# Magnitude tables as products of sixteen exponentials, a split of two long VectorE operations, late PSUM banks and new weights in a planner that orders a fused kernel on one core

## The chip, the cores and the metric

The kernel runs on one core of one Trainium2 chip. The metric is the device time of one execution in microseconds (us). A profile of one execution gives for every engine which instruction ran when: TensorE (PE, with its weight loads apart as PEld), VectorE (DVE), ScalarE (ACT), GpSimd (POOL, unused here) and SyncE (SP, which issues all DMAs of this kernel in one queue).

## The reference

The reference mixes two branches over one input x (2048 tokens, 512 channels), all in float32:

```python
g = sigmoid((x * gate_w).sum(-1, keepdims=True))
# a: a convolution along the tokens with a kernel K of length L = 2048 per channel d
dt   = exp(log_dt)[:, None]
P    = exp((dt * (A_re + 1j * A_im))[:, :, None] * arange(L))        # 512 x 128 x 2048
K    = einsum("dn,dnl,dn->dl", C, P, dt * B).real
a    = irfft(rfft(u padded to 2L) * rfft(K padded to 2L))[:L] + u * Dskip
# b: a gated MLP, hidden width 1792
b    = (sigmoid(x @ w_gate) * (x @ w_up)) @ w_down
out  = g * a + (1 - g) * b
```

What the change touches most is P. With the token index written as l = 32 i + j, each of the 512 x 128 complex powers is a product of a value at a multiple of 32 and a value at a small step, so K comes out of small matmuls over the 128 states instead of out of 512 x 128 x 2048 exponentials.

## The kernel before

**The MLP** takes most of TensorE. The tokens are worked in two halves of 1024, each in two blocks of 512; the hidden width in 14 slices of 128, in groups of 4, 4, 3 and 3. Inputs and weights are split into a high and a low part (`split`, L678: ACT copies the high part, DVE subtracts it, through four staging buffers `st`), and each product is three matmuls in float32r. `hidden` (L731) makes 24 matmuls a slice and block into two PSUM banks (`gups`, L749); `post` (L760) is the chain behind them: sigmoid on ACT (L764), product on DVE (L766), high part on ACT (L770), low part on DVE (L771). `down` (L782) multiplies by `w_down` (`dps`, L798), and `add` (L808) adds the result into an accumulator, on ACT for the first group (L814) and on DVE after (L817).

**The kernel K** is made in 16 groups of 32 channels, one after the other. `bases` (L281) computes for a group: the angles (DVE L315, ACT L317, DVE L318, ACT L331), cosine and sine (ACT L332 and L333) into the tile `ex`, five exponentials a channel and state on ACT for the doubling steps (`e5`, L334), and the magnitudes `mg` = exp(aa * q) for q = 0..63, a table of 32 x 64 values a partition. These are 32 ACT instructions, one a channel, with the channel's decay as a per-partition scale (`mags`, L336 to L338). `tables` (L365) then multiplies `mg` and `ex` into the table B (DVE L389 with 2048 elements, L392 and L393 with 1024), builds the table T by five doublings on DVE (L350 to L361), and 64 small matmuls (`kps`, L409) give K. `first` (L418) takes the first step of K's transform (ACT L422, DVE L425, matmuls `wps` L434, ACT L446) and stores every two groups (`a_k`). The tiles `ex`, `mg`, T and B have one buffer each, so the next group's `bases` starts when B is built, and T is refilled when the small matmuls have read it.

**The convolution** is a transform in steps: `rows` (L461) transforms the input and stores it (`a_u`); `passes` (L519) runs over two halves of the channels, each as soon as its eight groups of K are stored, with 16 steps (`step`, L543: matmuls `s2u` and `s2k`, products on DVE, matmuls `ips`, a store to `b_s`); `finals` and `last` (L602, L618) load `b_s` back, finish the transform (matmuls `fps`) and add it to the MLP's accumulator (DVE L640 and L647), from which the output is stored.

**The order of the work** is not written out. All these functions are generators ("strands"), each of which yields one operation at a time with its engine, a price and the times when its inputs are ready, and `Plan.run` (L150) merges them while the program is built: it keeps a clock for every engine, and always issues the operation with the smallest key, which is its possible start on that clock plus the strand's weight ("bias").

```python
                    start = max(ready, self.free.get(eng, 0.0))
                    key = start + st[0]
```

The prices are formulas: `dve(n)` = 0.067 + n x 1.042e-3 us and `act(n)` = 0.06 + n x 0.88e-3 us for n elements a partition. The merge decides the order on each engine for good; on the chip each engine works its instructions off in that order and waits where an input is late. A PSUM bank (three are shared by everything but the MLP, `XB`) is taken when the strand asks for it, which it does before its matmuls' inputs are ready.

Of the kernel before, what the change touches and what calls it, by code (L numbers as in the profile page):

```python
# [31 lines left out]
P = 128  # L32
# [6 lines left out]
NA = len(ANGLES)  # L39
GROUPS = [4, 4, 3, 3]  # L40
HALF = L // 2
LN2H, LN2L = 0.693145751953125, 1.42860682030941723212e-6
WIDTHS = [256, 256]


def constants():
# [15 lines left out]
    for k in range(32):  # L62
# [11 lines left out]
        "c_pw": f(np.concatenate([ANGLES, ANGLES[33:], np.arange(64)]), 1, NA + 69),  # L74
# [23 lines left out]
def slots(pool, tag, n, shape, dtype=F32):  # L98
    return [Slot(pool, f"{tag}{i}", shape, dtype) for i in range(n)]


class Plan:
# [47 lines left out]
    def run(self):  # L150
        while True:
            best = None
            i = 0
            while i < len(self.strands):
# [20 lines left out]
            if eng == "SP":  # L175
# [17 lines left out]
            fn(eng) if isinstance(st[2][0], tuple) else fn()  # L193
# [3 lines left out]
def body(ctx, tc, xp, xt, prm, ldt, dsk, gw, wgu, wdn, c_wu, c_wf, c_wk, c_ww, c_pw, out):  # L197
# [26 lines left out]
    GU, DN, XB = (slots(ps, n, k, [P, 512]) for n, k in (("gu", 3), ("dn", 2), ("xb", 3)))  # L224
# [6 lines left out]
    pw = cst.tile([P, NA + 69], F32, name="pw")  # L231
# [49 lines left out]
    def bases():  # L281
# [3 lines left out]
        for gi in range(NG):  # L285
# [11 lines left out]
            e5 = kp.tile([P, 5, 32], F32, tag="e5", name="e5")  # L297
# [5 lines left out]
            def first():  # L303
# [3 lines left out]
            sh = [P, 5, 32]  # L307
            te = yield "DVE", dve(160), lambda: V.tensor_tensor(
                e5, aa[:, 0:1].to_broadcast(sh), pw[:, NA:NA + 5, None].to_broadcast(sh), op=OP.mult), [t]
# [24 lines left out]
            te = yield "ACT", ("exp", act(160)), lambda: A.activation(e5, e5, AF.Exp), [te]  # L334

            def mags():  # L336
                for d in range(32):
                    A.activation(mg[:, d], pw[:, NA + 5:], AF.Exp, scale=aa[:, 0, d:d + 1])  # L338
            tm = yield "ACT", ("exp", 32 * act(64)), mags, [t]
# [5 lines left out]
                bz[:, 0::2], trig, e5[:, None].to_broadcast([P, 2, 5, 32]), op=OP.mult), [t, te, bzs.t]  # L345
# [19 lines left out]
    def tables():  # L365
        for gi in range(NG):
# [7 lines left out]
            def start():  # L374
# [25 lines left out]
            bzs.free(t)  # L400
            bank, = yield XB, 1
# [12 lines left out]
            plan.spawn(first(gi, j, p, bank, t), 0.0)  # L414
# [3 lines left out]
    def first(gi, j, p, bank, t):  # L418

        ks, = yield KST, 1  # L420
# [4 lines left out]
        t = yield "DVE", 0.2, lambda: V.tensor_tensor(kst[:, :, 0], kst[:, :, 0], dskt[:, gi], op=OP.add), [t, E["dsk"].t]  # L425
        banks = yield XB, 2
# [15 lines left out]
        for jh in range(2):  # L442
# [3 lines left out]
            te = yield "ACT", 0.9, lambda: [A.activation(dst[:, :, i], src[:, :, i], AF.Copy) for i in range(2)], [t, kv.t]  # L446
# [14 lines left out]
    def rows():  # L461
        yield E["wu"]
        yield E["gwb"]
        for t in range(NM):
# [12 lines left out]
            gate[t].set((yield "ACT", ("sig", 0.2), sig, [te]))  # L477
            banks = yield XB, 2
# [8 lines left out]
            plan.spawn(urest(t, ph, banks, tp), 0.1)  # L487
# [31 lines left out]
    def passes():  # L519
# [8 lines left out]
        for j in range(NW):  # L528
            yield kdone[j]
            for q in range(16):  # L530
# [9 lines left out]
                plan.spawn(step(j, q, ww, wws, au, ak, s2, max(tw, ta), max(tw, tk)), 0.1)  # L540
            plan.spawn(finals(j), 0.3)

    def step(j, q, ww, wws, au, ak, s2, ta, tk):  # L543
        w = WIDTHS[j]
        bank, = yield XB, 1
# [6 lines left out]
        bank.free(tu)  # L552
        bank, = yield XB, 1
# [20 lines left out]

        banks = yield XB, 2
# [26 lines left out]
    def finals(j):  # L602
        yield bdone[j]
        for m in range(0, NM, 2):
# [11 lines left out]
            plan.spawn(last(j, m, b, s2, max(tb)), 0.2)  # L616

    def last(j, m, b, s2, tb):  # L618
        w = WIDTHS[j]
        banks = yield XB, 2  # L620
# [57 lines left out]
    def split(src, hi, lo, slot, ready, parts, rest):  # L678
# [17 lines left out]
        plan.spawn(halves(), 0.0)  # L696
# [34 lines left out]
    def hidden():  # L731
        for half in range(2):
            f0 = 0
            for gn in GROUPS:
                for sb in range(2):
                    for f in range(f0, f0 + gn):
# [16 lines left out]
                        plan.spawn(post(half, sb, f, pp), 0.0)  # L753
# [141 lines left out]
```

## Time and profile before

| | us |
|---|---|
| median of 3 runs | 822.63 (821.9 to 825.05) |
| the profiled execution | 823.44 |
| its span, first to last instruction | 821.7 |
| PE busy | 708.2 |
| DVE busy | 537.1 |
| ACT busy | 496.6 |

The profile names a group of instructions by line, engine and operation with the tiles written and read, gives its busy time, the mean duration of one, and the idle time of its engine just before it, with what ended that idle time. Busy time of matmuls is modelled from starts, and holds the time in which they run at a lower clock. "L" numbers in everything taken from the kernel before are its lines; the changed kernel's lines are some 10 to 30 higher (L338 there was the magnitudes' ACT line, its DVE line is now L353; L749 is now L776, L798 is L825, L627 is L654, L686 is L713).

### The profile page before, as it was taken

What the parts mean: (1) busy time and instruction counts of PE and PEld (TensorE: products, weight loads), DVE (VectorE), ACT (ScalarE), POOL (GpSimd) and SP (SyncE); (2) the same over time, 40 slices, a digit from 0 to 9 for tenths busy, and PEclk for the clock granted to TensorE, in tenths of its full rate; (3) what the DMA queues carried; (4) which work ended last, traced back from release to release, by engine and by line L of the source; (5) the groups of instructions that cost most, each with busy time, mean ns of one, the idle gap of its engine ahead of it and who ended that gap; (6) DMA issues with size and microseconds to landing.
All of it is one profiled execution on the core that took longest, in us unless ns stands there. A gap on an engine that the chain in (4) does not pass through costs nothing.

```text
span 821.7 us, 15690 instructions
## 1 busy us (share of the span) xinstructions
PE 708.2 (86%) x6176; PEld 503.8 (61%) x6176; DVE 537.1 (65%) x1011; ACT 496.6 (60%) x1102; POOL 0.2 (0%) x4
## 2 busy tenths in 40 slices
PE   3869887888889988978898879897997989999997
PEld 1546555767668776756556555665676746566555
DVE  6658386887878876976586848666896444353332
ACT  4958939788587793677776867693966222222000
POOL 0000000000000000000000000000000000000000
PEclk9879898999999997998899999899999999999998
DMA  7883372920346264248156525694231755557541
GB/s 213 322 284 106 106 196 93 346 85 7 103 162 261 46 212 173 91 103 319 46 161 166 186 72 167 215 276 131 79 103 46 278 166 183 175 189 272 179 155 52
DMA packets 100490, 134.02 MB, mean 163 GB/s; under 512 B 42304, under 2 KB 65216, under 8 KB 96832
## 3 DMA queue, kind: packets, MB, share of 16 engines
q1 hardware_dynamic: 100416, 133.01, 50.1%
q8 instruction: 49, 0.80, 0.4%
q14 instruction: 25, 0.20, 0.1%
HBM read 79.50 MB, written 53.48 MB: 162 GB/s over the span
## 4 chain that ended last, share of the span: by engine, by line
PE 39%; ACT 33%; DMA 14%; DVE 7%; issue 3%; SPq 3%; DVEq 0%; ACTq 0%
PE gups L749 18%; ACT mg L338 14%; PE dps L798 8%; DMA au<-a_u 6%; PE ips L582 4%; PE s2u L513 2%; PE s2k L513 2%; ACT L334 2%; PE wps L434 2%; ACT L764 2%; PE ups L484 2%; ACT ex L332 2%; DMA al<-acc 2%; ACT mg L331 2%; ACT L332 2%
## 5 line engine op out<-in xcount | busy, mean ns | idle before, releaser
L749 PE MATMUL gups<-x,gu 128*128 128x512 f32 x1344 | 341.7, 407 | 10.4 <-DMA gu<-wsp 5.3
L749 PEld LDWEIGHTS gups<-x,gu 128*128 128x128 f32 x1344 | 257.8, 195 | 86.0 <-issue 17.8
L798 PE MATMUL dps<-dnw,h 128*128 128x512 f32 x672 | 187.9, 420 | 36.3 <-ACT h L770 28.9
L798 PEld LDWEIGHTS dps<-dnw,h 128*128 128x128 f32 x672 | 127.5, 198 | 89.5 <-ACT h L770 35.6
L338 ACT ACTIVATE mg<-pw,aa 128x64 f32<-128x64 f32 x512 | 124.1, 335 | 0.0
L766 DVE TENSOR_TENSOR gups<-gups,sg 128x512 f32<-128x512 f32 x56 | 39.1, 698 | 67.7 <-PE gups L749 43.5
L770 ACT ACTIVATE h<-gups 128x512 fp32r<-128x512 f32 x56 | 33.3, 594 | 65.9 <-DVE gups L766 65.9
L561 DVE TENSOR_TENSOR tt<-s2k,uf 128x512 f32<-128x512 f32 x32 | 22.1, 690 | 56.2 <-PE s2k L513 53.3
L771 DVE TENSOR_TENSOR h<-gups,h 128x512 fp32r<-128x512 f32 x56 | 38.5, 688 | 27.9 <-ACT h L770 27.2
L764 ACT ACTIVATE sg<-gups 128x512 f32<-128x512 f32 x56 | 33.5, 598 | 34.0 <-PE gups L749 33.6
L817 DVE SCALAR_TENSOR_TENSOR acc<-dps,omg,acc 128x512 f32<-128x512 f32 x48 | 35.9, 748 | 25.5 <-PE dps L798 25.3
L551 ACT ACTIVATE uf<-s2u 128x512 f32<-128x512 f32 x32 | 19.0, 595 | 49.2 <-PE s2u L513 41.6
L361 DVE TENSOR_TENSOR T<-T,t 128x64 f32<-128x64 f32 (+4 forms) x80 | 46.5, 581 | 1.8
L359 DVE TENSOR_TENSOR t<-T,bz 128x64 f32<-128x64 f32 (+4 forms) x80 | 46.2, 577 | 1.6
L513 PE MATMUL s2u<-au,ww 128*64 128x256 f32 x256 | 34.7, 390 | 14.3 <-DMA au<-a_u 13.8
L360 DVE TENSOR_TENSOR T<-T,bz 128x64 f32<-128x64 f32 (+4 forms) x80 | 46.0, 575 | 0.0
L446 ACT ACTIVATE kev<-wps 128x256 f32<-128x256 f32 x64 | 32.4, 666 | 21.1 <-PE wps L434 21.0
L589 ACT ACTIVATE ev<-ips 128x256 f32<-128x256 f32 x64 | 21.2, 380 | 37.9 <-PE ips L582 28.6
L582 PE MATMUL ips<-y,ww 64*128 64x256 f32 x256 | 37.7, 410 | 3.6 <-ACT ev L589 3.4
L409 PE MATMUL kps<-B,T 128*32 128x64 f32 x2048 | 33.6, 226 | 7.1 <-DVE T L361 5.8
L484 PE MATMUL ups<-u,wu 64*128 64x512 f32 x64 | 23.3, 771 | 18.7 <-DMA u<-xp 15.1
L409 PEld LDWEIGHTS kps<-B,T 128*32 128x32 f32 x2048 | 31.1, 114 | 13.4 <-issue 11.7
(81 smaller groups left out, 728.9 us busy)
## 6 DMA issues: line engine op xcount, KB each, us to landing
wsp<-gu SPq DMA_DIRECT2D x14, 1024.0 KB, 6.1
gu<-wsp SPq DMA_DIRECT2D x14, 1024.0 KB, 8.6
a_u<-evu SPq DMA_DIRECT2D x32, 256.0 KB, 3.5
a_k<-kev SPq DMA_DIRECT2D x8, 1024.0 KB, 6.9
ww<-c_ww SPq DMA_DIRECT2D x32, 256.0 KB, 2.8
au<-a_u SPq DMA_DIRECT2D x32, 256.0 KB, 3.4
ak<-a_k SPq DMA_DIRECT2D x32, 256.0 KB, 4.2
b_s<-ev SPq DMA_DIRECT2D x32, 256.0 KB, 4.2
```

Of the source, the lines that this page charges most:

```text
L338: A.activation(mg[:, d], pw[:, NA + 5:], AF.Exp, scale=aa[:, 0, d:d + 1])
L359: yield "DVE", dve(n), lambda: V.tensor_tensor(t2, src, sb, op=OP.mult), [t, slot.t]
L360: t = yield "DVE", dve(n), lambda: V.tensor_tensor(dst, src, br, op=OP.mult), [t]
L361: t = yield "DVE", dve(n), lambda: V.tensor_tensor(dst, dst, t2[:, :, ::-1], op=OP.add), [t]
L409: mm(p[32 * jj:32 * jj + 32, s], T[:, ch, c], B[:, ch, c], start=(c == 0), stop=(c == 1), tile_position=(0, 32 * jj), skip_group_check=True)
L484: mm(ph[jp], wu[r, jp], u[r], start=True, stop=True, tile_position=(64 * jp, 0))
L513: mm(p[64 * kb_:64 * kb_ + 64, c], ww[:, kb_, 64 * c:64 * c + 64], a(kb_), start=True, stop=True, tile_position=(0, 64 * kb_), skip_group_ ...
L582: mm(pi[i], ww[r, 2 + c], y[r, c], start=(c == 0), stop=(c == 1), tile_position=(64 * i, 0))
L749: mm(p, gu[:, a, k, dc], x[:, b, dc], start=(dc + n == 0), stop=(dc == NC - 1 and n == 2))
L764: t = yield "ACT", ("sig", act(512)), lambda: A.activation(sg, pg_, AF.Sigmoid), [tg, ss.t]
L766: t = yield "DVE", dve(512), lambda: V.tensor_tensor(pu, pu, sg, op=OP.mult), [t, tu]
L798: mm(p, h[:, a, 128 * s:128 * s + 128], dn[:, b], start=(f == f0 and n == 0), stop=(f == f0 + gn - 1 and n == 2))
```

## The change

Four things are changed.

- **Magnitudes.** q = 8 a + b, so exp(aa q) is a product of exp(aa 8 a) and exp(aa b). The tile `e5` of five exponents becomes `ep` with 21 (eight multiples of eight, eight units, and the five of before): one DVE product and one ACT exponential of 672 elements instead of 160. The table `mg` is made by two DVE products of 1024 elements each, which read both factors from `ep`, whose layout is exponent by channel.
- **Long DVE operations in two.** The product of 2048 elements into B becomes two of 1024; the magnitudes too are made in two.
- **Banks late.** A strand that is about to take a PSUM bank first yields a pseudo-operation (`near`) without an engine, whose key is the time at which its inputs are ready minus 0.48 us. Some strands also wait for an event earlier than before.
- **Weights.** All strands' weights are new numbers (`BIAS`), and the key has two new terms: half of the ACT table load that an operation would cause, and the mode switch on PE.

```diff
+POWERS = list(range(0, 64, 8)) + list(range(8)) + ANGLES[33:]
+NP = len(POWERS)
+BANKS = dict(gu=3, dn=2, xb=3)
+BIAS = dict(x=-0.91, w=0.02, split=-0.1, rows=-0.2, urest=1.37, bases=0.28, tables=0.33, first=0.42, hidden=0.92,
+            post=0.04, down=0.54, add=0.22, passes=-4.76, step=0.19, finals=0.41, last=0.41, const=1.21)
+CHANGE = dict(ACT=0.5, PE=1)
+EARLY = -0.48
...
-                    start = max(ready, self.free.get(eng, 0.0))
-                    key = start + st[0]
+                    start = max(ready, self.free.get(eng, 0.0)) - (m if eng is None else 0.0)
+                    key = start + st[0] + CHANGE.get(eng, 0.0) * (self.cost(eng, m) - (m[1] if isinstance(m, tuple) else m))
...
+    near = lambda *deps: (None, EARLY, None, list(deps))
...
-            e5 = kp.tile([P, 5, 32], F32, tag="e5", name="e5")
+            ep = kp.tile([P, NP, 32], F32, tag="ep", name="ep")
...
-            te = yield "DVE", dve(160), lambda: V.tensor_tensor(
-                e5, aa[:, 0:1].to_broadcast(sh), pw[:, NA:NA + 5, None].to_broadcast(sh), op=OP.mult), [t]
+            te = yield "DVE", dve(32 * NP), lambda: V.tensor_tensor(
+                ep, aa[:, 0:1].to_broadcast(sh), pw[:, NA:, None].to_broadcast(sh), op=OP.mult), [t]
...
-            te = yield "ACT", ("exp", act(160)), lambda: A.activation(e5, e5, AF.Exp), [te]
-
-            def mags():
-                for d in range(32):
-                    A.activation(mg[:, d], pw[:, NA + 5:], AF.Exp, scale=aa[:, 0, d:d + 1])
-            tm = yield "ACT", ("exp", 32 * act(64)), mags, [t]
+            te = yield "ACT", ("exp", act(32 * NP)), lambda: A.activation(ep, ep, AF.Exp), [te]
+
+            sh = [P, 16, 8, 8]
+            m8, m1 = (ep[:, i:i + 8].rearrange("p a d -> p d a") for i in (0, 8))
+            tm = max(t, te)
+            for d in (slice(0, 16), slice(16, 32)):
+                tm = yield "DVE", dve(1024), lambda: V.tensor_tensor(
+                    mg[:, d].rearrange("p d (a b) -> p d a b", b=8), m8[:, d, :, None].to_broadcast(sh),
+                    m1[:, d, None, :].to_broadcast(sh), op=OP.mult), [tm - 0.2]
...
-            sh = [P, 32, 2, 32]
-            yield "DVE", dve(2048), lambda: V.tensor_tensor(
-                B[:, :, :, 32:], ex[:, :, :, :32], mg[:, :, None, 32:].to_broadcast(sh), op=OP.mult), [tb]
+            sh = [P, 16, 2, 32]
+            for d in (slice(0, 16), slice(16, 32)):
+                yield "DVE", dve(1024), lambda: V.tensor_tensor(
+                    B[:, d, :, 32:], ex[:, d, :, :32], mg[:, d, None, 32:].to_broadcast(sh), op=OP.mult), [tb]
...
+            yield near(t, tb)
             bank, = yield XB, 1
             p = bank.tile("kps", [P, 8, 64])
...
-            plan.spawn(first(gi, j, p, bank, t), 0.0)
+            plan.spawn(first(gi, j, p, bank, t), BIAS["first"])
...
+        yield near(t)
         banks = yield XB, 2
         ph = [b.tile("wps") for b in banks]
...
+        yield near(ta)
         bank, = yield XB, 1
         p = bank.tile("s2u", [P, 2, w])
```

The two parts of the order that the prediction speaks of, beside the magnitudes themselves, are the start and the end of the program.

The first operations of ACT up to the first slice's last weight copy (`x` and `xt` are the MLP's input, `gu` and `dnw` its weights; `g` and `omg` the gate), before:

```order
L686 ACT_TABLE_LOAD
L686 ACTIVATE x<-st 128x512 x3
L686 ACTIVATE gu<-st 128x512
L475 ACT_TABLE_LOAD
L475 ACTIVATE g<-gl 128x1
L476 ACTIVATE omg<-gl 128x1
L686 ACTIVATE x<-st 128x512
L686 ACTIVATE gu<-st 128x512
L686 ACTIVATE x<-st 128x512
L686 ACTIVATE dnw<-st 128x512
```

and now:

```order
L713 ACTIVATE x<-st 128x512 x3
L713 ACTIVATE gu<-st 128x512
L713 ACTIVATE x<-st 128x512 x2
L496 ACT_TABLE_LOAD
L496 ACTIVATE g<-gl 128x1
L497 ACTIVATE omg<-gl 128x1
L713 ACTIVATE x<-st 128x512 x3
L713 ACTIVATE gu<-st 128x512
L496 ACTIVATE g<-gl 128x1
L497 ACTIVATE omg<-gl 128x1
L713 ACTIVATE dnw<-st 128x512
```

The first slice's weights (two `gu` and one `dnw`) were complete with the 8th staged copy, and are complete with the 11th, because all eight tiles of the first two input blocks go ahead.

The last rows of PE (`fps` is the last step of the convolution, eight of them for the second half of the channels), before:

```order
L627 MATMUL fps<-b_in,wf 32x256 x8
L749 MATMUL gups<-x,gu 128x512 x12
L627 MATMUL fps<-b_in,wf 32x256 x8
L749 MATMUL gups<-x,gu 128x512 x6
L798 MATMUL dps<-dnw,h 128x512 x3
L749 MATMUL gups<-x,gu 128x512 x24
L798 MATMUL dps<-dnw,h 128x512 x3
L749 MATMUL gups<-x,gu 128x512 x12
L798 MATMUL dps<-dnw,h 128x512 x30
```

and now:

```order
L776 MATMUL gups<-x,gu 128x512 x12
L654 MATMUL fps<-b_in,wf 32x256 x8
L776 MATMUL gups<-x,gu 128x512 x6
L654 MATMUL fps<-b_in,wf 32x256 x8
L825 MATMUL dps<-dnw,h 128x512 x12
L654 MATMUL fps<-b_in,wf 32x256 x8
L825 MATMUL dps<-dnw,h 128x512 x6
L654 MATMUL fps<-b_in,wf 32x256 x8
L825 MATMUL dps<-dnw,h 128x512 x12
L654 MATMUL fps<-b_in,wf 32x256 x8
```

Before, 78 MLP matmuls stand behind the last `fps`; now none does. Counted over the whole order, 2016 MLP matmuls (`gups` and `dps`) remain as they were; 1620 of them stood ahead of the last group's `kps` and 1797 ahead of the last `s2u`, now 1650 and 1902.

Around the second group's magnitudes on ACT, before (`ex` cosine and sine, `kst` and `kev` the first step of K's transform, `h` the MLP's hidden tile):

```order
L814 ACTIVATE acc<-dps,omg 128x512
L764 ACTIVATE sg<-gups 128x512
L338 ACT_TABLE_LOAD
L338 ACTIVATE mg<-pw,aa 128x64 x32
L475 ACT_TABLE_LOAD
L475 ACTIVATE g<-gl 128x1
L476 ACTIVATE omg<-gl 128x1
L446 ACTIVATE kev<-wps 128x8x32 x4
```

and the second group's magnitudes now, on DVE:

```order
L376 TENSOR_TENSOR T<-T,bz 128x64x16
L377 TENSOR_TENSOR T<-T,t_572 128x64x16
L793 TENSOR_TENSOR gups<-gups,sg 128x512
L353 TENSOR_TENSOR mg<-ep 128x1024
L798 TENSOR_TENSOR h<-gups,h 128x512
L353 TENSOR_TENSOR mg<-ep 128x1024
L491 SCALAR_TENSOR_TENSOR ju,gl<-u,gwb 128x512
L360 TENSOR_TENSOR bz<-ex,ep 128x2x160
```

The 32 instructions stood on ACT as one block; the two products stand on DVE with an operation of the MLP between them. ACT's table loads in the whole order are 58 now, and were 70.

More of the change, by code (lines that the diff above doesn't have):

```diff
@@ L174, in run @@
             _, st, eng, m, start = best
-            if eng == "SP":
+            if eng is None:
+                end = start
+            elif eng == "SP":
                 end = start + 0.4
@@ L192, in run @@
             fn = st[2][2]
-            fn(eng) if isinstance(st[2][0], tuple) else fn()
+            if fn is not None:
+                fn(eng) if isinstance(st[2][0], tuple) else fn()
             self.step(st, end)
@@ L477, in rows @@
             gate[t].set((yield "ACT", ("sig", 0.2), sig, [te]))
+            yield near(tu)
             banks = yield XB, 2
@@ L552, in step @@
         bank.free(tu)
+        yield near(tk)
         bank, = yield XB, 1
@@ L573, in step @@
         ts.free(t)
+        yield near(t)
         banks = yield XB, 2
@@ L695, in halves @@
                     yield from rest(te)
-        plan.spawn(halves(), 0.0)
+        plan.spawn(halves(), BIAS["split"])
     left = {}
@@ L804, in down @@
                                     plan.spawn(release(half, f, ds, t), 0.0)
-                        plan.spawn(add(half, gi, half * 8 + sb * 4 + s, p, bank, t), 0.0)
+                        plan.spawn(add(half, gi, half * 8 + sb * 4 + s, p, bank, t), BIAS["add"])
                 f0 += gn
```

41 lines of the change are left out of this document (23 added, 18 removed).

## The prediction

> **What bounds the kernel now.** I read the page's busy times and its chain of waits first.
>
> ```profile
> span 821.7 us, 15690 instructions
> PE 708.2 (86%) x6176; PEld 503.8 (61%) x6176; DVE 537.1 (65%) x1011; ACT 496.6 (60%) x1102; POOL 0.2 (0%) x4
> PE 39%; ACT 33%; DMA 14%; DVE 7%; issue 3%; SPq 3%; DVEq 0%; ACTq 0%
> PE gups L749 18%; ACT mg L338 14%; PE dps L798 8%; DMA au<-a_u 6%; PE ips L582 4%; PE s2u L513 2%; PE s2k L513 2%; ACT L334 2%; PE wps L434 2%; ACT L764 2%; PE ups L484 2%; ACT ex L332 2%; DMA al<-acc 2%; ACT mg L331 2%; ACT L332 2%
> ```
>
> PE is the fullest engine, but it stands idle for 821.7 - 708.2 = 113.5 us, and the chain that ended last runs for 33% on ACT. Its second line is L338, the magnitudes: 14% of 821.7 us is 115 us. So the question is which of PE's idle time goes. The view of waits, PE alone:
>
> ```profile
> PE dps L798 <- ACT h L770: 28.9, 13, 6.9
> PE ups L484 <- DMA u<-xp: 15.1, 4, 10.7
> PE s2u L513 <- DMA au<-a_u: 13.8, 12, 1.7
> PE wps L434 <- DVE kst L425: 9.6, 5, 4.3
> PE kps L409 <- DVE T L361: 5.8, 4, 3.8
> PE gups L749 <- DMA gu<-wsp: 5.3, 1, 5.3
> PE dps L798 <- DVE h L771: 3.9, 13, 1.0
> PE ups L484 <- ACT kev L446: 3.7, 1, 3.7
> PE ips L582 <- ACT ev L589: 3.4, 1, 3.4
> PE dps L798 <- ACT acc L814: 3.4, 1, 3.4
> PE gups L749 <- ACT sg L764: 2.8, 1, 2.8
> PE gups L749 <- ACT gu L686: 2.0, 1, 2.0
> PE kps L409 <- ACT ev L589: 1.3, 1, 1.3
> ```
>
> The ten rows that name ACT or DVE add up to 64.8 us; the three of DMA to 34.2 us. The timeline shows how the ACT rows come about; this is the longest wait, first ACT, then PE:
>
> ```profile
> 37.15 7.75 ACT L338 ACTIVATE mg<-pw,aa 128x64 f32<-128x64 f32 x32
> 48.99 0.60 ACT L770 ACTIVATE h<-gups 128x512 fp32r<-128x512 f32 x1 [0.74 <-DVE gups L766]
> 49.64 0.80 PE L798 MATMUL dps<-dnw,h 128*128 128x512 f32 x1 [6.87 <-ACT h L770]
> ```
>
> The magnitudes hold ACT for 7.75 us in one piece, the MLP's sigmoid (L764) and copy (L770) queue behind, and PE waits 6.87 us. The kernel's own merge did not foresee it: its price for the 32 instructions is 32 x act(64) = 32 x 0.116 = 3.72 us, and the chip takes 124.1 / 16 = 7.76 us (row L338 below). Each group's block ends 4.04 us later than the order was laid out for, 65 us in all, about as much as PE waits for ACT and DVE. That is no proof, but it is my main reason: the order is fixed, so lateness is paid wherever it has no slack.
>
> **The change part by part.** The groups view with shapes apart gives durations:
>
> ```profile
> L338 ACT ACTIVATE mg<-pw,aa 128x64 f32<-128x64 f32 x512 | 124.1, 335 | 0.0
> L764 ACT ACT_TABLE_LOAD x22 | 28.2, 1283 | 0.4
> L331 ACT ACTIVATE mg<-ex 128x1216 f32<-128x1216 f32 x16 | 19.5, 1221 | 12.6 <-DVE ex L318 12.6
> L334 ACT ACTIVATE e<-e 128x160 f32<-128x160 f32 x16 | 5.4, 337 | 0.2
> L392 DVE TENSOR_TENSOR B<-mg,ex 128x1024 f32<-128x1024 f32 x16 | 19.5, 1218 | 0.0
> L304 DVE TENSOR_TENSOR aa<-pg,dt 128x64 f32<-128x64 f32 x16 | 3.5, 217 | 0.0
> L344 DVE TENSOR_TENSOR bz<-ex,e 128x320 f32<-128x320 f32 x16 | 11.6, 725 | 1.9 <-ACT e L334 1.9
> L378 DVE TENSOR_TENSOR w<-w,ex 128x64 f32<-128x64 f32 x16 | 4.4, 273 | 0.6
> L359 DVE TENSOR_TENSOR t<-T,bz 128x128 f32<-128x128 f32 x16 | 4.7, 292 | 0.5
> ```
>
> ACT loses 124.1 us. It gains 512 more elements in each exponential, at (1221 - 337) / (1216 - 160) = 0.84 ns each 0.43 us, 6.9 us in 16 groups. Twelve table loads fewer are 12 x 1.283 = 15.4 us. ACT falls to 496.6 - 124.1 + 6.9 - 15.4 = 364 us and stops being a suspect.
>
> DVE gains. A plain product costs (1218 - 217) / (1024 - 64) = 1.043 ns an element plus 0.15 us. The longer product for `ep` adds 512 x 1.043 = 0.53 us a group, the split of B 0.07 us (the fixed part of the planner's price; at most the rows' own, 0.15). The two new products have no row. Lower bound: a plain product, 1.218 us. But their second factor is read with a step of 32 elements (128 bytes) from one element to the next. Rows that read an operand with a wide step are dearer: L344 takes 725 ns for 320 elements where the plain line gives 150 + 334 = 484, and L378 takes 273 for 64 where L304 takes 217. That is (725 - 150) / 320 = 1.80 and (273 - 150) / 64 = 1.92 ns an element. L359 reads pairs of neighbours and pays nothing (292 against 150 + 133). So the upper bound is 0.15 + 1024 x 1.92 = 2.1 us; I take 0.15 + 1024 x 1.80 = 2.0 us, because only the step tells those rows from plain ones, and the new products have it.
>
> [...]
>
> DVE's gain is then 16 x (2 x 2.0 + 0.53 + 0.07) = 74 us, most of it before the last group. Whether it fits is read from the windows:
>
> ```profile
> 0.00:643.95 643.95, 548.31 (x5076) 397.83 (x5077) 471.36 (x892) 461.56 (x1027) 0.20 (x4) 0.94 0.50 160
> 643.95:821.70 177.75, 159.88 (x1100) 105.98 (x1100) 65.76 (x120) 35.04 (x75) 0.00 (x0) 0.99 0.54 174
> 240.00:280.00 40.00, 39.40 (x352) 32.05 (x350) 33.51 (x63) 29.31 (x64) 0.00 (x0) 1.00 0.50 185
> ```
>
> 643.95 us is the start of the last `kps`. Up to there DVE works 471 us, 73%; with the change 545 us. PE's 548 us are matched: two engines of nearly the same load that feed each other. The fullest of the 40 us slices, the third row, had DVE at 84%.
>
> The terms, against the profiled execution's 823.4 us (its median is 822.6, so no correction):
>
> *Waits of PE for ACT and DVE, 64.8 us.* The new products are priced dve(1024) = 1.13 us, 0.08 under a plain row, as all DVE prices are; what is dearer than plain is lateness, 2 x (2.0 - 1.22) = 1.6 us a group instead of 4.04, 60% less. Since it now sits on a fuller engine, and the 0.69 us operations of the MLP queue behind 2 us products, I take half: -32 us. Ends: none, and 60 us.
>
> *Slow matmuls after a wait.* The timeline has the same six `dps` at two speeds:
>
> ```profile
> 524.56 2.92 PE L798 MATMUL dps<-dnw,h 128*128 128x512 f32 x6 [3.40 <-ACT acc L814]
> 667.15 1.66 PE L798 MATMUL dps<-dnw,h 128*128 128x512 f32 x6
> ```
>
> After a wait of 3.4 us they take 1.26 us more, in busy time and not in idle time. The rows above name seven waits of ACT or DVE that are certain to be this long (the longest of L798 on h, kst, T, kev, ev, acc, sg); I take half away at 1.3 us: -5 us. Ends 0 and -10.
>
> [...]
>
> *Start.* Three more staged copies stand ahead of the first slice's weights. The DMA issues of the 5th, 8th and 9th copy and of the 12th:
>
> ```profile
> 9.13 0.34 SPq L682 DMA_DIRECT2D st<-xt  x1
> 10.75 0.33 SPq L682 DMA_DIRECT2D st<-wdn  x1
> 15.57 0.64 SPq L682 DMA_DIRECT2D st<-xt  x1
> 17.83 0.38 SPq L682 DMA_DIRECT2D st<-wgu  x1
> ```
>
> Four buffers turn round in about 6.4 us (9.13 to 15.57), 1.6 us a copy, so the first `gups` come up to 4.8 us later. Later slices need fewer copies; I take +4 us. Ends 0 and 5.
>
> *End.* Before, the last eight `fps` ran from 764.85 to 794.86 us,
>
> ```profile
> 764.85 0.66 PE L627 MATMUL fps<-b_in,wf 64*32 64x256 f32 x16
> 794.86 1.28 PE L627 MATMUL fps<-b_in,wf 64*32 64x256 f32 x16
> ```
>
> 30 us with 75 MLP matmuls among them, and 78 behind. Now 69 are among them and none behind. Each waits for loads whose buffers the `fps` two before it frees. Their cover is thinner; I take +3 us. Ends 0 and 10.
>
> *Late banks, weights, mode and table terms of the key* move instructions and add none; their worth is in the waits above, and I give no term of its own. DMA waits stay at 34 us: the same transfers are issued, but for a smaller `pw`.
>
> Sum: 823.4 - 32 - 5 + 4 + 3 = 793.4; I say **793 us**. As a check, L338's 115 us of the chain become 16 x (2 x 2.0 + 0.43) = 71 us, which frees 44 us of it at most along that way.
>
> **The rivals.**
>
> *DVE becomes the bound.* DVE's 545 us before the last `kps` can't be packed tighter than its fullest slice, 84%: 545 / 0.84 = 649 us, 5 us later than now. Behind it remain 177.75 us less the 30 MLP matmuls that now stand ahead of it (1.66 us for six, row above, so 8 us): 649 + 170 = 819 us of span. Some waits behind it go too; I put it at 816 us. For it: the load is in the rows. Against: in that same slice PE was busy for 39.4 of 40 us, so a DVE at 84% starves nobody.
>
> *PE is the bound and nearly all waits go*, if the new products are plain (1.22 us) and the new weights fit: 823.4 - 60 - 10 + 7 = 760 us. For it: the other prices are near their rows (dve(1024) = 1.13 against 1.218, act(1216) = 1.13 against 1.221). Against: the steps of 128 bytes.
>
> *Slower: the end.* If the groups finish no earlier than at 644 us, as the first rival says, and the `fps` with no MLP work behind them wait for their loads, each of the last four pays a round trip of issue and landing uncovered, some 2 to 3 us: +10, with +4 at the start: 823.4 + 4 + 10 - 5 = 832 us. It decides once the last `kps` starts after about 640 us. Against: the weights put 105 more MLP matmuls ahead of the last `s2u`, so less is left to do then.
>
> *The change doesn't do what it says*: not likely, as the 512 instructions are gone from the order.
>
> **How the numbers follow.** The forecast (770 to 810 us) gets 0.52, DVE as the bound (810 to 822) 0.2, PE as the bound (755 to 770) 0.16, the slower end 0.12. Range 758 to 822 us: below lies part of PE's case, above it the slower one and a tail of DVE's. Three runs of before spread by 0.4%, so I count under 0.5% (4 us) as no change: 818.5 is the border to faster. Faster: 0.52 + 0.16 + 0.12 of DVE's case = 0.80; same 0.09 (the rest of it, and 0.01 of the last), slower 0.11.
>
> **What would show it.** The two products' rows near 2.0 us each (plain 1.2 would prove the step harmless here). PE's waits for ACT at a third of their 46 us, PE's for DVE about where they are (19 us). The last `kps` between 610 and 630 us. The first `gups` 3 to 5 us later than before. A DVE share over 85% before the last `kps` with PE still waiting for it would mean the first rival; a last stretch with `fps` waiting for `b_in` for more than 8 us the slower one. If PE's waits for ACT stay although L338 is gone, the lateness was not their cause and my main term is wrong.

## The result: 9.3% faster, more than forecast

The changed kernel takes 747.85 us (745.69 to 749.12, 4 runs), the kernel before 823.84 us (821.9 to 828.92, 4 runs): a ratio of 0.9066, 95% interval 0.9018 to 0.9114. The forecast was 793 us with a range of 758 to 822; it had the sign and missed the size by 45 us.

The page of the changed kernel, busy times and the chain that ended last:

```profile
span 746.7 us, 15212 instructions
PE 680.0 (91%) x6176; PEld 490.9 (66%) x6176; DVE 590.0 (79%) x1043; ACT 374.9 (50%) x594; POOL 0.2 (0%) x4
PE 45%; DVE 22%; DMA 13%; ACT 12%; issue 5%; SPq 1%; DVEq 0%; ACTq 0%
PE gups L776 20%; PE dps L825 9%; DVE mg L353 6%; PE ips L607 4%; DMA au<-a_u 4%; PE s2u L535 4%; PE s2k L535 3%; DMA al<-acc 2%; DMA st<-wdn 2%; PE kps L427 2%; DVE gups L793 2%; DMA u<-xp 2%; PE ups L506 2%; ACT L345 2%; PE wps L455 1%
```

The span fell by 75.0 us. PE does the same 6176 matmuls, but in 680.0 instead of 708.2 us; its idle time fell from 113.5 to 66.7 us. So 47 us are idle time and 28 us are matmuls that run faster. The second part goes with the granted clock, here in the view of the cores (span and mean granted TensorE clock), of before and of after:

```profile
core 0: 821.7 us, clock 0.949
```

```profile
core 0: 746.7 us, clock 0.981
```

(1 - 0.949) x 821.7 = 42 us of clock withheld before, (1 - 0.981) x 746.7 = 14 us after. The difference, 28 us, is as large as PE's gain in busy time, but the two are not the same thing: the mean also counts stretches in which PE is idle. The records of the clock in both traces show full and half clock (1.0 and 0.5) alone. Before, 17 stretches at half clock add up to 83 us, and PE is busy for 69 us of them; after, 7 stretches add up to 28 us, with PE busy for 23. This is one of them, which sets in during the wait of 6.87 us for `h` that the prediction shows (stretch in us from the start, its length, busy us of PE, PEld, DVE, ACT and POOL with their instructions, granted clock, busy share of the DMA engines, GB/s):

```profile
45.55:55.79 10.24, 5.98 (x13) 3.28 (x13) 8.59 (x16) 4.61 (x12) 0.00 (x0) 0.50 0.62 234
```

In another stretch at half clock, 523.41 to 530.24 us, lies the slow one of the two rows of six `dps` that the prediction shows: 2.92 us, against 1.66 at 667.15 us, where the granted clock is 1.00, so 1.8 times as long. If a matmul takes twice as long at half clock, half of 69 - 23 = 46 us, some 23 of the 28 us, is the clock (at 1.8 times 20); this is an estimate, and what the other 5 us are is open.

PE's longest waits in the changed kernel (us, times, longest):

```profile
PE ups L506 <- DMA u<-xp: 15.3, 2, 12.7
PE dps L825 <- ACT h L797: 9.1, 6, 4.2
PE s2u L535 <- DMA au<-a_u: 5.5, 7, 1.6
PE fps L654 <- issue: 5.3, 3, 2.1
PE kps L427 <- ACT evu L517: 5.1, 1, 5.1
PE dps L825 <- DVE h L798: 4.7, 10, 0.9
PE gups L776 <- DMA gu<-wsp: 2.4, 1, 2.4
```

The wait for the MLP's `h` on ACT fell from 28.9 to 9.1 us, those for `kst` and T from 15.4 to under 3, and that for `au` from 13.8 to 5.5 us, though the same loads are issued.

The groups view of after has the two products. Behind it stand the windows up to and behind the end of the last `kps`, first of before, then of after with one slice of 40 us (columns as above); they show VectorE:

```profile
L353 DVE TENSOR_TENSOR mg<-ep 128x1024 f32<-128x1024 f32 x32 | 65.3, 2055 | 6.7 <-ACT ep L347 6.6
```

```profile
0.00:645.90 645.90, 550.26 (x5205) 399.69 (x5205) 471.82 (x892) 461.56 (x1027) 0.20 (x4) 0.94 0.50 161
645.90:821.70 175.80, 157.94 (x975) 104.12 (x972) 65.31 (x119) 35.04 (x75) 0.00 (x0) 0.99 0.53 171
```

```profile
0.00:583.10 583.10, 529.82 (x5174) 391.05 (x5175) 526.45 (x926) 339.54 (x517) 0.20 (x4) 0.98 0.56 179
583.10:746.70 163.60, 150.19 (x1009) 99.85 (x1006) 63.50 (x117) 35.41 (x77) 0.00 (x0) 0.98 0.58 181
480.00:520.00 40.00, 38.84 (x324) 29.32 (x323) 39.17 (x67) 24.68 (x27) 0.00 (x0) 1.00 0.59 178
```

The last group's `kps` end at 583 us instead of 646. VectorE is busy for 90% of the time up to there (73% before) and for 98% of the slice at 480 us, while PE works 97% of it.

### The profile page after: what moved, and what is told of

It is laid out like the page before. It is cut to its first block, busy times and chain, and to the rows that moved or that the text cites. A ratio compares the mean times of both kernels' runs of the same rounds, so it can differ in the third digit from the quotient of the medians.

```text
span 746.7 us, 15212 instructions
## 1 busy us (share of the span) xinstructions
PE 680.0 (91%) x6176; PEld 490.9 (66%) x6176; DVE 590.0 (79%) x1043; ACT 374.9 (50%) x594; POOL 0.2 (0%) x4
## 4 chain that ended last, share of the span: by engine, by line
PE 45%; DVE 22%; DMA 13%; ACT 12%; issue 5%; SPq 1%; DVEq 0%; ACTq 0%
PE gups L776 20%; PE dps L825 9%; DVE mg L353 6%; PE ips L607 4%; DMA au<-a_u 4%; PE s2u L535 4%; PE s2k L535 3%; DMA al<-acc 2%; DMA st<-wdn 2%; PE kps L427 2%; DVE gups L793 2%; DMA u<-xp 2%; PE ups L506 2%; ACT L345 2%; PE wps L455 1%
## 5 line engine op out<-in xcount | busy, mean ns | idle before, releaser
L776 PE MATMUL gups<-x,gu 128*128 128x512 f32 x1344 | 333.2, 399 | 4.0 <-DMA gu<-wsp 2.4
L776 PEld LDWEIGHTS gups<-x,gu 128*128 128x128 f32 x1344 | 251.7, 191 | 77.0 <-issue 18.9
L825 PE MATMUL dps<-dnw,h 128*128 128x512 f32 x672 | 178.6, 407 | 13.8 <-ACT h L797 9.1
L825 PEld LDWEIGHTS dps<-dnw,h 128*128 128x128 f32 x672 | 124.0, 191 | 61.5 <-issue 15.3
L353 DVE TENSOR_TENSOR mg<-ep 128x1024 f32<-128x1024 f32 x32 | 65.3, 2055 | 6.7 <-ACT ep L347 6.6
L427 PE MATMUL kps<-B,T 128*32 128x64 f32 x2048 | 33.7, 225 | 7.5 <-ACT evu L517 5.1
L406 DVE TENSOR_TENSOR B<-ex,mg 128x1024 f32<-128x1024 f32 x32 | 38.2, 1219 | 0.0
```

The source lines that it names most:

```text
L353: tm = yield "DVE", dve(1024), lambda: V.tensor_tensor(mg[:, d].rearrange("p d (a b) -> p d a b", b=8), m8[:, d, :, None].to_broadcast(sh) ...
L406: yield "DVE", dve(1024), lambda: V.tensor_tensor(B[:, d, :, 32:], ex[:, d, :, :32], mg[:, d, None, 32:].to_broadcast(sh), op=OP.mult), [tb]
L427: mm(p[32 * jj:32 * jj + 32, s], T[:, ch, c], B[:, ch, c], start=(c == 0), stop=(c == 1), tile_position=(0, 32 * jj), skip_group_check=True)
L776: mm(p, gu[:, a, k, dc], x[:, b, dc], start=(dc + n == 0), stop=(dc == NC - 1 and n == 2))
L825: mm(p, h[:, a, 128 * s:128 * s + 128], dn[:, b], start=(f == f0 and n == 0), stop=(f == f0 + gn - 1 and n == 2))
```

## The experiments

All times are medians; the kernel before ran beside each at 820.5 to 823.0 us. Differences are taken between the medians; taken from the ratios they come out up to 5 us otherwise. The runs fall into four questions.

### Was lateness against the plan the cost?

My main reason was that the 32 exponentials ran 4.04 us longer than priced. **The true price in the kernel before:**

```diff
-            tm = yield "ACT", ("exp", 32 * act(64)), mags, [t]
+            tm = yield "ACT", ("exp", 32 * 0.2424), mags, [t]
```

> The kernel before, unchanged but for one number in the planner: the 32 exponentials are priced 32 x 0.2424 = 7.76 us, as the profile measured them, instead of 3.72. If lateness against the plan was the cost (my theory), the order has room for the block and the time falls to 785 to 800 us. If the load on ScalarE was the cost whatever its price, 815 us or more.

821.72 us, ratio 0.9971 (0.9941 to 1.0000): no gain. The merge answered by putting 1782 instead of 1620 MLP matmuls ahead of the last group, so this run alone could hide a gain behind a bare end (too little MLP work left to cover the last steps of the convolution). The next takes that away, by **weighting the K strands 0.15 lower as well:**

```diff
-                      ... (bases(), 0.2), (tables(), 0.5), ...
+                      ... (bases(), 0.05), (tables(), 0.35), ...
```

> The kernel before with the exponentials priced as measured (as the second run) and the two strands that make K weighted 0.15 lower, so that 432 MLP matmuls stand behind the last group (234 in the second run, 396 in the kernel before) and the convolution's last step stands where it did. If lateness against the plan is what the ScalarE block costs, and the second run only lost it again in an uncovered end: 775 to 795 us. If the block's length costs, priced or not: 810 us or more.

837.06 us, ratio 1.0173 (1.0097 to 1.0249). With an honest price and enough work left for the end it is slower by 1.7%, with the whole interval above 1. PE's wait for `h` on ACT, 28.9 us in the kernel before, is 24.5 us in the first of the two runs and 33.7 us in the second: the price does not take it away. Each run was to bring over 20 us if lateness against the plan was the cost, and neither shows any of it. They are two orders out of many, and orders of the same work differ by 12 to 36 us further down, so that some order might gain by the true price is not excluded.

**The same order, a shorter block:** the kernel before with 8 ACT instructions of 256 elements a group in the place of 32 of 64 (the price, and so the order, stay).

```diff
-                for d in range(32):
-                    A.activation(mg[:, d], pw[:, NA + 5:], AF.Exp, scale=aa[:, 0, d:d + 1])
+                for d in range(0, 32, 4):
+                    A.activation(mg[:, d:d + 4], pw[:, None, NA + 5:].to_broadcast([P, 4, 64]), AF.Exp, scale=aa[:, 0, d:d + 1])
```

> The kernel before with its order unchanged on every engine, but a group's magnitudes made by 8 ScalarE instructions of 256 elements instead of 32 of 64, some 3.2 us, about what the planner priced (3.72) instead of 7.76. Left out: four neighbouring channels share the first one's decay, so three quarters of the magnitudes are not the right ones. Same order, same price, no lateness: if lateness was the cost, half or more of the 64.8 us of waits goes, 780 to 795 us. If the order itself is what costs, 805 to 823 us.

770.95 us, ratio 0.9364 (0.9331 to 0.9396): 51 us less. The group's row, the windows up to and behind the last `kps`, and PE's wait for `h`:

```profile
L338 ACT ACTIVATE mg<-pw,aa 128x256 f32<-128x256 f32 x128 | 53.2, 499 | 0.0
```

```profile
0.00:588.10 588.10, 530.47 (x5204) 389.62 (x5204) 471.58 (x892) 392.48 (x643) 0.20 (x4) 0.97 0.55 177
588.10:765.90 177.80, 160.34 (x987) 105.23 (x975) 65.38 (x119) 35.02 (x75) 0.00 (x0) 0.98 0.54 169
```

```profile
PE dps L798 <- ACT h L770: 15.4, 8, 3.2
```

ACT lost 124.1 - 53.2 = 71 us, and the program 51 us: 0.7 us of time for each us of block. The last `kps` came 58 us earlier. This block is short and also no longer late, so the run by itself does not tell the two apart. With the two runs before it, it says that the block's length in ACT's queue costs, also in orders that were laid out for it.

**The block back in the changed kernel's order,** as 32 exponentials of 59 elements behind the factors' exponential, into a tile that nobody reads:

```diff
+            du = kp.tile([P, NA + NP], F32, tag="du", name="du")
+
+            def exps():
+                A.activation(ep, ep, AF.Exp)
+                for d in range(32):
+                    A.activation(du, pw, AF.Exp, scale=aa[:, 0, d:d + 1])
-            te = yield "ACT", ("exp", act(32 * NP)), lambda: A.activation(ep, ep, AF.Exp), [te]
+            te = yield "ACT", ("exp", act(32 * NP)), exps, [te]
```

> The changed kernel with its order unchanged on every engine, and 32 exponentials of 59 elements a group added on ScalarE behind the exponential of the factors, into a tile that nobody reads and without a price: ScalarE gets its block of some 7.7 us back, as pure queueing. If the block on ScalarE costs by blocking the MLP's chain behind it: 775 us or more. If ScalarE has the room (50% busy): under 760 us.

905.63 us, ratio 1.1020 (1.0989 to 1.1052). The block came out longer than I meant it, 12.0 us a group: the 32 exponentials, which all write one tile, did not overlap (344 ns each, 11.0 us busy and 1.0 us idle a group), while those of before, each into its own part of `mg`, did (335 ns each, 7.76 us for the 32).

```profile
L352 ACT ACTIVATE du<-pw,aa 128x59 f32<-128x59 f32 x512 | 175.9, 344 | 16.2
```

```profile
PE dps L831 <- ACT h L803: 57.2, 7, 14.4
PE ups L512 <- ACT evu L523: 25.2, 4, 11.9
PE gups L782 <- ACT sg L797: 21.5, 3, 11.8
```

Busy and idle time of that row together, 192 us of block made 158 us of time, 0.8 each, though nothing reads its result and ACT was busy for only 547 of 903 us. What stands behind it in the queue is what PE needs next: all of PE's waits for ACT rise from 19 to 153 us. Here 93 us of clock are withheld by the mean of 0.897, and PE is busy for only 25.5 us more than in the changed kernel (705.5 us).

### What are the products worth without a new order?

**The products in the place of the exponentials,** in the kernel before, order unchanged on PE and ACT otherwise:

```diff
-                for d in range(32):
-                    A.activation(mg[:, d], pw[:, NA + 5:], AF.Exp, scale=aa[:, 0, d:d + 1])
+                for d in (slice(0, 16), slice(16, 32)):
+                    V.tensor_tensor(<mg, half d>, <m8>, <m1>, op=OP.mult)      # shortened; as in the changed kernel
```

The table of the factors grows to 672 elements here too.

> The kernel before with its order unchanged on every engine, but the 32 exponentials of a group left out and the two products issued on VectorE at the same place of the program. It prices the magnitudes without any new order. By the runs so far (71 us less of the ScalarE block gave 52, 27 us of VectorE's work gave 16): -124 x 0.73 + 74 x 0.6 = -46, 777 us; by my forecast's terms for it (-37): 786 us; by the first run (products under old weights, new order): 803 us.

819.11 us, ratio 0.9968 (0.9930 to 1.0005): no gain. What ACT gives, VectorE takes.

```profile
0.00:640.80 640.80, 549.76 (x5201) 402.61 (x5204) 541.19 (x924) 340.59 (x509) 0.20 (x4) 0.94 0.51 162
```

```profile
PE kps L414 <- DVE T L366: 25.9, 12, 4.2
PE dps L803 <- ACT h L775: 19.7, 9, 5.5
```

PE's wait for `h` falls to 19.7 us, and its wait for the table T rises from 5.8 to 25.9: the doublings now queue behind the products, as I read it. In all rows of the view, PE's waits for ACT fall from 46 to 21 us and those for DVE rise from 21.5 to 44. That products with packed factors would do better at this order was not run.

**With the merge free to reorder, under the old weights** (early banks, B whole):

> The kernel before with the magnitudes as products and nothing else of the change (old weights, banks taken early, the product of 2048 elements whole). If the time went with the magnitudes themselves (their late block on ScalarE), most of the 76 us is here: 760 to 780 us. If the new weights and late banks found the gain, little is here: 800 us or more.

802.84 us, ratio 0.9737 (0.9683 to 0.9792). The windows, up to and behind the last `kps`:

```profile
0.00:655.30 655.30, 577.66 (x5391) 426.69 (x5391) 551.00 (x941) 346.39 (x518) 0.20 (x4) 0.96 0.51 161
655.30:802.60 147.30, 119.84 (x789) 71.08 (x786) 53.37 (x102) 29.05 (x65) 0.00 (x0) 0.88 0.63 192
```

The merge put 1806 of 2016 MLP matmuls ahead of the last group, and the stretch behind it holds 120 us of PE work in 147 us at a clock of 0.88. **With the K strands weighted 0.1 lower** (`bases=0.1, tables=0.4`; 1620 ahead):

> The products alone (as the first run of this study), with the weights of the two strands that make K 0.1 lower, so that 396 MLP matmuls stand behind the last group's small matmuls instead of 210 (the kernel before: 396, the changed one: 366). If the first run lost its gain because too little MLP work was left to cover the end: 765 to 785 us, with TensorE's idle time after the last group at 15 us instead of 27. If not: 795 us or more.

795.60 us, ratio 0.9665 (0.9618 to 0.9712). Behind the last `kps` idle time fell from 27 to 13 us as expected, but the total by 7 us only: the earlier stretch idles 83 of 625 us instead of 78 of 655. The bare end was part of it, not the whole, and the 765 to 785 us that I expected did not come.

### What are the order's other parts worth?

**All but the magnitudes** (exponentials on ACT, at their true price):

> The changed kernel with the magnitudes back as 32 exponentials on ScalarE, priced as measured (7.76 us); late banks, new weights and the split kept. If weights and banks are the cause: 745 to 765 us. If the magnitudes are: 790 us or more. If lateness alone: about as the kernel before with the true price.

787.09 us, ratio 0.9551 (0.9512 to 0.9590). **All but the weights** (the old ones, without the two new terms of the key):

```diff
-BIAS = dict(x=-0.91, w=0.02, split=-0.1, rows=-0.2, urest=1.37, ...)
-CHANGE = dict(ACT=0.5, PE=1)
+BIAS = dict(x=0.0, w=0.0, split=0.0, rows=0.0, urest=0.1, ...)      # as before; constants 0.25
+CHANGE = dict()
```

> The changed kernel with the weights of before and without the key's terms for tables and modes; products, late banks and the split kept. If the new weights are worth much: 770 us or more. If the products carry it: 748 to 758 us.

783.66 us, ratio 0.9547 (0.9506 to 0.9587):

```profile
0.00:623.60 623.60, 561.11 (x5301) 411.23 (x5301) 547.24 (x950) 348.25 (x518) 0.20 (x4) 0.96 0.52 167
623.60:784.90 161.30, 138.43 (x877) 87.48 (x876) 58.61 (x109) 31.51 (x69) 0.00 (x0) 0.92 0.57 183
```

Against the changed kernel the weights are worth 36 us: PE idles 62 instead of 53 us up to the last `kps`, 23 instead of 13 behind it, and its busy time is 699.5 instead of 680.0 us at the lower clock. **All but the late banks** (`near` yields an event that has happened):

> The changed kernel with the banks taken as early as before (the pseudo-operation does nothing); all else kept. If late banks are worth much: 765 us or more; if not: 745 to 755 us.

754.83 us, ratio 0.9207 (0.9177 to 0.9237): 7 us. Under the old weights the late banks and the split together were worth more: 803 us without them (products only), 784 us with them (all but the weights).

**All but the split, at the changed kernel's order** (the 2048 elements in the place of the second half):

> The changed kernel with its order unchanged on every engine, but the product into B made whole (2048 elements, 2.28 us) in the place of the second half, nothing in that of the first. It prices the split alone: 745 to 751 us if an operation twice as long in the queue costs nothing, 753 us or more if the MLP's operations behind it wait.

751.40 us, ratio 0.9143 (0.9077 to 0.9209); the intervals overlap, so the split by itself is not told from nothing.

### Is the new order a region or a single point?

Four kernels do the changed kernel's work with one number of the merge moved: each product priced 0.2 us, or 1.97 us (near the true one), `hidden` 0.89 for 0.92, `tables` 0.31 for 0.33. A fifth nudges the kernel before (`hidden` 0.97 for 1.0).

> The changed kernel with each of the two products priced 0.2 us instead of 1.13, so that a group is about 3.7 us later than planned instead of 1.8 (before the change it was 4.0). If lateness costs about what I charged (half a microsecond of wait per microsecond of lateness): 16 x 1.9 x 0.5 = 15 us more, 760 to 770 us. If lateness is harmless: 745 to 752 us.

778.19 us, ratio 0.9433 (0.9380 to 0.9486).

> The changed kernel with the products priced 1.97 us as measured instead of 1.13, nothing else. If the remaining lateness of 1.7 us a group costs: 738 to 743 us. If it doesn't (VectorE is the bound and the price can't help), 745 to 752 us.

769.70 us, ratio 0.9383 (0.9343 to 0.9424): the better price makes it slower. The windows show where:

```profile
0.00:606.20 606.20, 567.48 (x5348) 420.88 (x5352) 541.72 (x945) 345.88 (x527) 0.20 (x4) 0.99 0.54 174
606.20:763.50 157.30, 117.95 (x832) 69.83 (x832) 51.51 (x99) 29.91 (x67) 0.00 (x0) 0.86 0.58 182
```

Up to the last `kps` this order keeps PE fuller: it idles 39 us there, in the changed kernel 53. But 1824 MLP matmuls stand there already, and the stretch behind has 118 us of PE work in 157 us.

> The changed kernel with one weight nudged (hidden 0.89 instead of 0.92), the same work: 1704 MLP matmuls ahead of the last group and 1980 ahead of the last s2u, instead of 1650 and 1902. If the merge's result is robust: 745 to 755 us. If the weights single out one good order and the end goes uncovered beside it: 760 to 780 us, with most of the loss behind the last group.

763.52 us, ratio 0.9286 (0.9244 to 0.9329); 26 us idle behind the last `kps`, 13 in the changed kernel.

> The changed kernel with another weight nudged (tables 0.31 instead of 0.33), the same work: 1656 MLP matmuls ahead of the last group (1650), 1926 ahead of the last s2u (1902). If the new weights are good as a region: 745 to 753 us. If they are one lucky order: 757 us or more, like the first nudge (763.5).

759.76 us, ratio 0.9246 (0.9171 to 0.9321).

> The kernel before with one weight nudged (hidden 0.97 instead of 1.0), the same work. If the old weights were an ordinary choice, their neighbour is as good: 815 to 835 us. If the kernel before sat on a bad draw: 800 us or less.

828.35 us, ratio 1.0071 (1.0031 to 1.0112): by this one neighbour, the kernel before was no unlucky draw.

All four neighbours of the changed kernel are slower than it, by 12 to 30 us, and all are faster than the old weights with the same work (784). So the new weights lie in a better region, and within it on an order that nothing near it reached here. Over all these orders the stretch behind the last `kps` was 147 to 185 us long, and never shorter than 147 with however little work:

| kernel | MLP matmuls left behind the last group | stretch, us | PE idle in it, us |
|---|---|---|---|
| true price of products | 192 | 157 | 39 |
| products only | 210 | 147 | 27 |
| true price, before | 234 | 156 | 29 |
| old weights | 300 | 161 | 23 |
| changed kernel | 366 | 164 | 13 |
| before | 396 | 176 | 18 |
| products priced 0.2 | 432 | 172 | 9 |

That its floor comes from the convolution's loads and stores is argued from this table, not tested by itself.

### Does VectorE set the time now?

**The factors packed:** the tile `ep` laid out channel by exponent, so that neighbours in the product are neighbours in memory. Prices and order stay.

```diff
-            ep = kp.tile([P, NP, 32], F32, tag="ep", name="ep")
+            ep = kp.tile([P, 32, NP], F32, tag="ep", name="ep")
-            m8, m1 = (ep[:, i:i + 8].rearrange("p a d -> p d a") for i in (0, 8))
+            m8, m1 = (ep[:, :, i:i + 8] for i in (0, 8))
```

> The changed kernel with the tile of 21 exponents laid out channel by exponent, so that the products read both factors from neighbouring elements; all else is the same. The products' rows should fall from 2.06 us to about 1.22 (if the step of 128 bytes makes them dear). VectorE loses 32 x 0.84 = 27 us. If VectorE, 92 to 98% busy up to the last group, is the bound there, the time falls by 10 to 25 us, to 723 to 738; if TensorE is, by less than 5 us.

731.79 us (728.45 to 732.33), ratio 0.8916 (0.8881 to 0.8951): better than both kernels.

```profile
L353 DVE TENSOR_TENSOR mg<-ep 128x1024 f32<-128x1024 f32 x32 | 38.5, 1218 | 5.5 <-ACT ep L347 5.5
L360 DVE TENSOR_TENSOR bz<-ex,ep 128x320 f32<-128x320 f32 x16 | 13.1, 816 | 0.0
```

The 2.055 us become 1.218, a plain product; the small product of `bz`, whose second factor is now read at a step of 21 elements (84 bytes), goes from 728 to 816 ns. 25 us less on VectorE gave 16 us. The shorter products are also nearer to their price of 1.13 us, which this run does not tell apart from the shorter work.

**One of the two products on GpSimd** on top of that:

```diff
-                tm = yield "DVE", dve(1024), lambda: V.tensor_tensor(
+                tm = yield "DVE", dve(1024), lambda: (V if d.start == 0 else nc.gpsimd).tensor_tensor(
```

> The packed version (732 us) with its order unchanged and the second of the two products of a group on GpSimd, which is idle, instead of VectorE: VectorE loses another 16 x 1.22 = 20 us. At the rate of the packed version (27 us less gave 16) 12 us less, 720 us, if GpSimd takes no longer than VectorE; if its product takes over 3 us, B waits for it: 740 us or more.

735.58 us, ratio 0.8962 (0.8940 to 0.8984): no gain.

```profile
L353 POOL TENSOR_TENSOR mg<-ep 128x1024 f32<-128x1024 f32 x16 | 43.5, 2722 | 496.6 <-ACT ep L347 475.1 <-DVE o L667 21.5
L353 DVE TENSOR_TENSOR mg<-ep 128x1024 f32<-128x1024 f32 x16 | 25.2, 1572 | 5.9 <-ACT ep L347 5.9
```

These are means of two kinds. In ten of the 16 groups VectorE's product starts just ahead of GpSimd's and takes its 1.22 us, and GpSimd's takes 3.0; in four it starts while GpSimd's runs and takes 2.4 to 2.9 us. One group of each kind:

```profile
106.29 1.23 DVE L353 TENSOR_TENSOR mg<-ep 128x1024 f32<-128x1024 f32 x1 [0.25 <-ACT ep L347]
106.39 3.00 POOL L353 TENSOR_TENSOR mg<-ep 128x1024 f32<-128x1024 f32 x1 [30.26 <-ACT ep L347]
201.62 2.02 POOL L353 TENSOR_TENSOR mg<-ep 128x1024 f32<-128x1024 f32 x1 [21.18 <-ACT ep L347]
201.80 2.92 DVE L353 TENSOR_TENSOR mg<-ep 128x1024 f32<-128x1024 f32 x1
```

Other VectorE products took longer in this run too (at 241.73 us a doubling `t<-T,bz` of 1024 elements 3.00 us instead of 1.22; the 16 `bz` products 1285 ns on average instead of 816). In sum VectorE is busy for 565.6 us with all 32 products on it and for 565.6 us with 16 of them on GpSimd: nothing was taken off it.

## Why the prediction was wrong

- **"Late banks, weights, mode and table terms ... I give no term of its own." This is the step that failed.** With the other parts in place the weights are worth 36 us, most of the 45 that I missed, and the late banks 7 us. I put their worth into the waits that the magnitudes would free. But the magnitudes free nothing by themselves (819 us at an unchanged order), and the new order without them brings 36 us (787). Together they bring 76: as I read it, the products take the long block from ACT, and the new order makes use of it on a VectorE that is now full.
- **The waits for ACT and DVE, -32, measured about -40: near, and by luck.** In all rows of the view PE's waits for ACT fell from 46 to 19 us and those for DVE from 21.5 to 9. The size was drawn from lateness and from the products, and the products alone leave the sum of the two where it was (68 and 65 us). The sign that I named for my main term, that PE's waits for ACT should fall, came; it did not single out lateness.
- **Lateness, the main reason, was not borne out.** The two runs with a true price (822 and 837 us) say so, as far as two orders can. That 65 us of lateness stood against 65 us of waits was a coincidence. The block's length in an in-order queue was the cost, 0.7 to 0.8 us of time for each us of block at a fixed order.
- **Slow matmuls, -5 us, measured -28: the largest single miss in the sum.** I counted seven waits at 1.3 us. The records of the clock have 17 stretches at half clock before and 7 after, and PE is busy in 69 and 23 us of them, which by the estimate above makes some 23 of the 28 us. With the old weights and all else of the change PE is still busy for 699.5 us, 19.5 more than in the changed kernel.
- **The products at 2.0 us: right** (2.055), and the packed layout shows the reason, the step of 128 bytes: without it the same product took 1.218 us.
- **VectorE "can't be packed tighter than its fullest slice, 84%": wrong.** It ran at 90% up to the last `kps` and 98% in a slice, with PE at 97% and waiting for DVE less than before. A share seen under one order is no limit of the engine. VectorE also gained 53 us (537.1 to 590.0) and not the 74 that I added up, in part because the new order does 16 of the 18 `evu` copies that VectorE did before, some 0.69 us each, on ACT. Yet VectorE was near the bound, as the rival said: 25 us less gave 16.
- **Start +4, measured about +1:** the first `gups`, before and after,

```profile
18.04 7.42 PE L749 MATMUL gups<-x,gu 128*128 128x512 f32 x24
```

```profile
19.34 5.91 PE L776 MATMUL gups<-x,gu 128*128 128x512 f32 x18
```

- **End +3:** PE's idle time before the `fps` rose from 4.0 to 6.5 us; about right. But the last `kps` came at 583 us, not at 610 to 630. The slower rival's bare end did not come in the changed kernel, but it did in the variants whose merge ran the MLP too far ahead (39 us idle with the products' true price).
- **DMA waits "stay": they fell** by 11 us in the three rows quoted (34.2 to 23.2), most of it before `s2u`. In all rows that name a DMA it is 38 to 24 us. It goes with the weights: 24 us with the new ones and the old exponentials, 34 with the old ones and the products. Not every order of the new weights has it (35 us with the products' true price), and which placement of the loads brings it is open.

The rival with PE as the bound, 760 us, came nearest. It would have needed plain products, which did not hold; what carried the time there was the order, so that its nearness is luck.

## What to carry to other kernels

Where a search or a planner's weights set the order, the order is a part of the change with a price of its own: here 36 us at equal work, and 12 to 30 us lost again by nudging one number. The operation that moved between two in-order engines here was worth nothing until the order was made anew, and the long block in such a queue cost 0.7 to 0.8 of its length though its engine was 40 to 50% idle. Before estimating what fewer waits will save, look at how much work runs at the lower clock. The clock that is withheld, (1 - granted clock) x span, says that something is there, but it overstates the work lost where PE is idle at the lower clock: with the block back on ACT 93 us were withheld, and PE was busy for 25.5 us more than in the changed kernel.

## What the runs showed of the hardware

- With one operand read at a step of 128 bytes, a VectorE product of 1024 float32 elements took 2.055 us against 1.218 us packed, 0.82 ns an element more.
- With one of a group's two products on GpSimd and the other on VectorE, the one that started while the other ran took longer: 2.4 to 2.9 us on VectorE (1.22 where it started first) and 3.0 us on GpSimd (2.0 to 2.3 in five of the six groups in which it started first). VectorE's whole busy time did not fall by the 16 products that GpSimd took over (565.6 us with them and without).
- 32 ScalarE exponentials into 32 different parts of a tile took 7.76 us (335 ns each, overlapping); 32 of nearly the same size into one and the same tile took 12.0 us (344 ns each, not overlapping). That the shared tile is the reason is argued, not tested.
- The granted clock was full or half (1.0 or 0.5 in every record of the two traces, before and after). In the kernel before the half came in stretches of 3.4, 6.8 or 10.2 us, and 15 of the 17 set in during a wait of PE of 2.0 us or more, or within 2 us of its end.
